# Linear attention and two gated layers on one Trainium2 core: features divided by their denominators before they are turned, and attention products of rounded parts and remainders with up to 512 moving columns

## The chip, the cores and the metric

The kernel runs on one core of a Trainium2 chip. The metric is the device time of one execution in microseconds; before the change it was 1078.28 us, the median of three runs (1075.19 to 1078.71).

## The reference

Attention with random features over 4 batches, 8 heads, 576 tokens, 64 dimensions and 128 features, and then two gated layers over all 2304 tokens (512 wide, 1536 inside), all in float32:

```
def phi(x):
    proj = np.einsum('bhsd,md->bhsm', x, omega)
    h = proj - np.sum(x * x, axis=-1, keepdims=True) / 2.0
    h = h - np.max(h, axis=-1, keepdims=True)
    return np.exp(h) / np.sqrt(m)
q_p, k_p = phi(q * scale), phi(k * scale)
kv = np.einsum('bhsm,bhsd->bhmd', k_p, v)
z = np.sum(k_p, axis=2)
num = np.einsum('bhsm,bhmd->bhsd', q_p, kv)
den = np.einsum('bhsm,bhm->bhs', q_p, z)[..., None] + 1e-06
x = num / den            # then the heads side by side: 2304 tokens x 512
x = (silu(x @ w_gate) * (x @ w_val)) @ w_out
out = ((x @ w_a) * (x @ w_b)) @ w_out2
```

## The kernel before

The 2304 tokens are cut into five chunks: four of 512 and one of 256 tokens. A batch has 576 tokens, so the second chunk holds the last 64 tokens of batch 0 and 448 of batch 1, the third 128 and 384, the fourth 192 and 320, the last one 256 of one batch. Activations lie with the features on the partitions and the tokens as columns, so that each layer's product has the weights as the stationary operand and up to 512 tokens as moving columns.

Precision comes from splitting. A float32 operand is split into a rounded part of the type fp32r (a "hi", written by ScalarE) and the remainder (a "lo", written by VectorE, line 307), and a product of two such operands is three fp32r products: hi by hi, hi by lo and lo by hi (lines 582 to 584). The attention before the change doesn't split its features: there the products of features and key sums are plain fp32 (lines 421 and 486). In the trace a plain fp32 product leaves two records.

`keys` computes, for a batch and a pair of heads, the features of the keys and their product with the values (with a column of ones beside them, so that the last of 65 columns is z): `kvs`. `queries` computes for a chunk and a pair of heads the features of the queries (`qf`), turns them by a transpose on TensorE (line 466) into PSUM, copies them to `fT` (ScalarE, line 469), multiplies each token tile and head by `kvs` (line 486; a tile that crosses from one batch to the next is multiplied by both), adds eps to column 65, takes the reciprocal and scales (VectorE, lines 503, 507, 511) into `xt`, and turns `xt` back (line 519). `put` splits the result into `xh` and `xl`, the first layer's input. `features` is used by both: GpSimd squares the tokens (line 341) and writes the remainder of the projection's input (line 307, tile `rl`); VectorE sums the squares and finds the row maximum; ScalarE takes the exponential.

`weights` provides the stationary operands. In the first chunk (c = 0) each block of weights is rebuilt from 64-bit numbers, by two ScalarE and two VectorE operations (lines 542 to 551), kept in DRAM, and then split (lines 562 and 565). In the later chunks it is loaded and only split. Seven blocks of split weights have buffers.

All instructions are first recorded, each with an engine, a cost, a due time and the tiles that it reads and writes. A planner (class `Plan`) then goes through a modelled time, and on each engine takes, of what is ready, what is due first; tiles of a ring are given out in the order of recording. What comes out is a fixed order on each engine, and an engine stops at an instruction whose inputs are late. The attention of the next chunk is due between two thirds of this chunk's first layer and nine tenths of its second, so the second chunk's attention lies in the first chunk, among its weights' rebuilding. ScalarE has to load a table when it goes from exponential to silu or back.

## Time and profile before

| | |
|---|---|
| median of three runs | 1078.28 us |
| the profiled execution's own time | 1075.15 us |
| its span, first to last instruction | 1073.4 us |
| TensorE busy | 1053.0 us |
| VectorE busy | 659.4 us |
| ScalarE busy | 605.0 us |
| GpSimd busy | 87.5 us |
| granted clock of TensorE | 1.00 |

TensorE's busy time is made of instructions that overlap, so a full engine says that it always had one under way, and not how fast they followed each other; the chain of waits, which counts each instruction from the end of the one before it, tells the pace. Shares of the whole span hide that the first chunk, up to about 290 us, differs from what follows: there the weights are rebuilt.

### The profile page before, as it was taken

Reading aid. Unit: us, or ns where it says so; the run is one execution under the profiler, and the core shown is the slowest. Engines: PE = TensorE matmul, PEld = TensorE weight load, DVE = VectorE, ACT = ScalarE, POOL = GpSimd, SP = SyncE. Lnnn points to the kernel's source line nnn. Section 1 sums busy time; section 2 is a strip of 40 time slices with the busy share of each in tenths; the row PEclk is TensorE's granted clock in tenths of the full one; section 3 lists DMA queues with packets and bytes.
Section 4 is the critical chain, followed back from the end, with each engine's and each line's share of the span. In section 5 each row is a group of like instructions: output and inputs, shape, how many; then the busy total and the mean of one; then the engine's idle time right before and its main releaser. Section 6 shows DMA issues by size and latency. Waiting matters only on the chain.

```text
span 1073.4 us, 15791 instructions
## 1 busy us (share of the span) xinstructions
PE 1053.0 (98%) x5596; PEld 900.6 (84%) x5596; DVE 659.4 (61%) x1266; ACT 605.0 (56%) x1212; POOL 87.5 (8%) x73
## 2 busy tenths in 40 slices
...
GB/s 269 247 274 239 259 310 259 277 281 257 186 108 98 89 133 103 101 125 132 118 99 95 101 93 101 84 73 104 112 97 101 96 89 90 89 118 183 183 184 99
DMA packets 113263, 162.59 MB, mean 151 GB/s; under 512 B 30112, under 2 KB 53280, under 8 KB 113184
## 3 DMA queue, kind: packets, MB, share of 16 engines
...
q14 instruction: 35, 0.29, 0.1%
HBM read 137.95 MB, written 23.59 MB: 151 GB/s over the span
## 4 chain that ended last, share of the span: by engine, by line
PE 80%; DVE 12%; ACT 5%; issue 2%; DMA 1%; POOL 0%; SPq 0%; ACTq 0%; DVEq 0%; POOLq 0%
PE ps_m L582 24%; PE ps_m L584 23%; PE ps_m L583 23%; PE ps_p L373 3%; DVE w L548 2%; PE ps_t L486 2%; DVE wl L307 2%; PE ps_kv L421 2%; DVE w L551 2%; DVE mx L379 1%; PE ps_t L466 1%; ACT w L545 1%; ACT w L542 1%; DVE s L346 1%; ACT wh L562 1%
## 5 line engine op out<-in xcount | busy, mean ns | idle before, releaser
L307 DVE TENSOR_TENSOR wl<-w,wh 128x512 fp32r<-128x512 f32 x360 | 258.6, 720 | 247.6 <-ACT wh L562 242.4
L582 PE MATMUL ps_m<-xh,wh 128*128 128x512 f32 (+1 forms) x960 | 360.1, 375 | 3.1 <-ACT wh L562 1.2
L583 PE MATMUL ps_m<-xl,wh 128*128 128x512 f32 (+1 forms) x960 | 353.8, 369 | 0.8 <-DVE xl L307 0.8
L584 PE MATMUL ps_m<-xh,wl 128*128 128x512 f32 (+1 forms) x960 | 354.4, 369 | 0.1
L562 ACT ACTIVATE wh<-w 128x512 fp32r<-128x512 f32 x360 | 226.0, 631 | 177.7 <-PE ps_m L583 134.4
L582 PEld LDWEIGHTS ps_m<-xh,wh 128*128 128x128 f32 x960 | 181.3, 189 | 31.0 <-ACT a L600 1.6
L584 PEld LDWEIGHTS ps_m<-xh,wl 128*128 128x128 f32 x960 | 181.0, 189 | 31.2 <-DVE wl L307 0.5
L583 PEld LDWEIGHTS ps_m<-xl,wh 128*128 128x128 f32 x960 | 181.3, 189 | 28.6 <-DVE xl L307 1.2
L582 PE MATMUL ps_m<-hh,wh 128*128 128x512 f32 (+1 forms) x480 | 181.4, 378 | 0.0
L584 PE MATMUL ps_m<-hh,wl 128*128 128x512 f32 (+1 forms) x480 | 177.6, 370 | 0.2 <-DVE wl L307 0.2
L583 PE MATMUL ps_m<-hl,wh 128*128 128x512 f32 (+1 forms) x480 | 177.0, 369 | 0.0
L600 ACT ACTIVATE a<-ps_m 128x512 f32<-128x512 f32 (+1 forms) x120 | 66.7, 556 | 98.2 <-PE ps_m L584 97.6
L603 DVE TENSOR_TENSOR h<-a,ps_m 128x512 f32<-128x512 f32 (+1 forms) x120 | 75.8, 632 | 60.2 <-PE ps_m L584 54.0
L584 PEld LDWEIGHTS ps_m<-hh,wl 128*128 128x128 f32 x480 | 90.5, 189 | 16.7 <-DVE wl L307 1.1
L582 PEld LDWEIGHTS ps_m<-hh,wh 128*128 128x128 f32 x480 | 90.7, 189 | 13.0 <-ACT wh L562 0.2
L583 PEld LDWEIGHTS ps_m<-hl,wh 128*128 128x128 f32 x480 | 90.7, 189 | 13.0
L606 ACT ACTIVATE hh<-h 128x512 fp32r<-128x512 f32 (+1 forms) x120 | 70.9, 591 | 26.6 <-DVE h L603 24.6
L307 DVE TENSOR_TENSOR hl<-h,hh 128x512 fp32r<-128x512 f32 (+1 forms) x120 | 77.9, 649 | 7.1 <-ACT hh L606 2.1
L307 POOL TENSOR_TENSOR rl<-qT,rh 128x512 fp32r<-128x512 f32 (+1 forms) x16 | 20.4, 1275 | 615.1 <-ACT rh L354 516.3
L393 ACT ACTIVATE qf<-ps_p,bias 128x128 f32<-128x128 f32 x144 | 42.3, 377 | 29.7 <-DVE bias L387 29.5
L379 DVE TENSOR_REDUCE mx<-ps_p 128x4 f32<-128x512 f32 (+1 forms) x72 | 46.1, 641 | 16.0 <-PE ps_p L373 15.4
L548 DVE SCALAR_TENSOR_TENSOR w<-w 128x512 uint32<-128x512 uint32 x72 | 51.8, 725 | 6.6 <-ACT w L545 6.4
...
## 6 DMA issues: line engine op xcount, KB each, us to landing
...
```

The lines of the kernel that those rows point to most:

```text
L307: eng.tensor_tensor(out=out, in0=a, in1=hi.bitcast(F32), op=ALU.subtract)
L373: nc.tensor.matmul(out, lhsT=w, rhs=x, start=j == 0, stop=j == len(terms) - 1)
L379: on(DVE, dve(256 * n), d, lambda ps=ps, mx=mx, n=n: nc.vector.tensor_reduce(out=mx.tile[:, 0:n], in_=ps.tile.rearrange("p (t h m) -> p t ...
L393: nc.scalar.activation(out=f.tile[:, g + i, h], in_=ps.tile[:, 256 * i + M * h:256 * i + M * (h + 1)], func=AF.Exp, scale=qk_scale, bias=b ...
L548: on(DVE, dve(CW), due - 9, lambda: nc.vector.scalar_tensor_tensor(out=raw.tile[:, :, 0], in0=raw.tile[:, :, 1], scalar=0x80000000, in1=ra ...
L562: on(ACT, act(CW), due - 7, lambda: nc.scalar.activation(out=hi.tile.rearrange("p a c -> p (a c)"), in_=w.tile, func=AF.Copy), reads=[(w,) ...
L582: nc.tensor.matmul(o, lhsT=hi.tile[:, wi], rhs=a, start=first, stop=False)
L583: nc.tensor.matmul(o, lhsT=hi.tile[:, wi], rhs=b, start=False, stop=False)
L584: nc.tensor.matmul(o, lhsT=lo.tile[:, wi], rhs=a, start=False, stop=last)
L600: on(ACT, act(n, 0, True), due, lambda a=a, ps=ps: nc.scalar.activation(out=a.tile[:, 0:n], in_=ps[0].tile[:, 0:n], func=AF.Silu if m == 0 ...
L603: on(DVE, dve(n), due, lambda a=a, h=h, ps=ps: nc.vector.tensor_tensor(out=h.tile[:, 0:n], in0=a.tile[:, 0:n], in1=ps[1].tile[:, 0:n], op= ...
L606: on(ACT, act(n), due + 2, lambda h=h, hh=hh: nc.scalar.activation(out=hh.tile[:, 0:n], in_=h.tile[:, 0:n], func=AF.Copy), reads=[(h,)], w ...
```

## The change

From the second chunk on (`split` is true) `queries` goes to a new function `shared`; the first chunk keeps the way of before (`own`, which now turns the features by head and borrows its tiles from other rings). In `shared`, z is first widened for each batch and pair (`widen`): a column of z, repeated 128 times, is transposed on TensorE, so that z stands in a row on all partitions (`zb`). GpSimd multiplies the features by `zb` (`weigh`), VectorE sums the products to the denominator, adds eps and takes the reciprocal, and GpSimd multiplies the features by it in place. Only then are they turned, each head's four tiles into one PSUM tile, and split into `fh` (ScalarE) and `fl` (VectorE). The key sums are split too (`kp`, with a block of zeros between the two heads, so that a stationary operand of 128 columns holds one head and zeros). Six fp32r products for each batch add both heads into one PSUM tile that has the layout of x, with the batch's tokens of the chunk as moving columns. No transpose of the result follows.

Buffers change with it: keys' and queries' inputs share three tiles; the squares are written over the tokens; the layers' temporaries `a`, `h` and `o` share three tiles; `hh` and `hl` have one tile less. The planner's cost of an fp32 product of 65 columns goes from 0.15 to 0.233.

```diff
--- before.py
+++ after.py
@@ -246,17 +246,16 @@
     ps_k = ring("ps_kv", 1, [P, 512], space=PSUM)
 
     ones = Fixed(None)
+    zeros = Fixed(None)
     ident = fixed("ident", [P, P])
     bd = fixed("bd", [P, 2 * M])
     bdh = fixed("bdh", [P, 2 * M], F32R)
     bdl = fixed("bdl", [P, 2 * M], F32R)
 
-    r_kT = ring("kT", 2, [P, S])
+    r_kT = r_qT = ring("xT", 3, [P, S])
     r_kt = ring("kt", 1, [P, KT, P])
-    r_qT = ring("qT", 2, [P, NT])
     r_qt = ring("qt", 1, [P, NT // P, P])
     r_vt = ring("vt", 2, [P, KT, 2, VA])
-    r_sq = ring("sq", 1, [P, KT, 2, D])
     r_s = ring("s", 3, [P, KT, 2])
     r_nsq = ring("nsq", 3, [P, KT, 2])
     r_rh = ring("rh", 1, [P, S], F32R)
@@ -267,17 +266,18 @@
     r_kf = ring("kf", 1, [P, KT, 2, M])
     r_qf = ring("qf", 2, [P, NT // P, 2, M])
     r_kvs = ring("kvs", 9, [P, 2, VA])
-    r_fT = ring("fT", 1, [P, 2, NT])
-    r_den = ring("den", 3, [P, 2, 2])
-    r_rec = ring("rec", 3, [P, 2, 2])
-    r_xt = ring("xt", 1, [P, NT // P, 2, D])
+    r_zb = ring("zb", 9, [P, 2, M])
+    r_kp = ring("kp", 2, [P, 2, 3, D], F32R)
+    r_fh = ring("fh", 2, [P, NT], F32R)
+    r_fl = ring("fl", 2, [P, NT], F32R)
+    r_pr = ring("pr", 1, [P, 2, 2, M])
+    r_den = ring("den", 3, [P, NT // P, 2])
+    r_rec = ring("rec", 3, [P, NT // P, 2])
     r_xh = ring("xh", 9, [P, NT], F32R)
     r_xl = ring("xl", 9, [P, NT], F32R)
-    r_a = ring("a", 2, [P, NT])
-    r_h = ring("h", 2, [P, NT])
-    r_hh = ring("hh", NF + 1, [P, NT], F32R)
-    r_hl = ring("hl", NF + 1, [P, NT], F32R)
-    r_o = ring("o", 2, [P, NT])
+    r_a = r_h = r_o = ring("tmp", 3, [P, NT])
+    r_hh = ring("hh", NF, [P, NT], F32R)
+    r_hl = ring("hl", NF, [P, NT], F32R)
     r_w64 = ring("w64", 4, [P, CW, 2], U32)
     r_w32 = ring("w32", 4, [P, CW])
     r_wh = ring("wh", 7, [P, NG, P], F32R)
...
@@ -337,15 +340,15 @@
     def features(rT, tok, nt, step, f, due, length, split, psum):
 
         width = step * (nt - 1) + P
-        sq, s, nsq = r_sq.buf(), r_s.buf(), r_nsq.buf()
-        on(POOL, pool(nt * P), due - 4, lambda: nc.gpsimd.tensor_tensor(
-            out=sq.tile[:, 0:nt].rearrange("p t h d -> p (t h d)"),
-            in0=tok.tile[:, 0:nt].rearrange("p t c -> p (t c)"),
-            in1=tok.tile[:, 0:nt].rearrange("p t c -> p (t c)"), op=ALU.mult),
-            reads=[(tok,)], writes=[(sq,)])
+        s, nsq = r_s.buf(), r_nsq.buf()
+
+        def square():
+            x = tok.tile[:, 0:nt].rearrange("p t c -> p (t c)")
+            nc.gpsimd.tensor_tensor(out=x, in0=x, in1=x, op=ALU.mult)
+        on(POOL, pool(nt * P), due - 4, square, writes=[(tok,)])
         on(DVE, dve(nt * P), due - 2, lambda: nc.vector.tensor_reduce(
-            out=s.tile[:, 0:nt], in_=sq.tile[:, 0:nt], op=ALU.add, axis=AX.X),
-            reads=[(sq,)], writes=[(s,)])
+            out=s.tile[:, 0:nt], in_=tok.tile[:, 0:nt].rearrange("p t (h d) -> p t h d", h=2),
+            op=ALU.add, axis=AX.X), reads=[(tok,)], writes=[(s,)])
         on(DVE, dve(16), due - 2, lambda: nc.vector.tensor_scalar(
             out=nsq.tile[:, 0:nt], in0=s.tile[:, 0:nt], scalar1=sq_scale, scalar2=None,
             op0=ALU.mult), reads=[(s,)], writes=[(nsq,)])
...
@@ -417,7 +420,7 @@
         for t in range(KT):
             for h in range(2):
                 r = rows[t]
-                on(PE, pe(0.15), due + length * (t + 1) / KT, lambda h=h, t=t, r=r:
+                on(PE, pe(0.233), due + length * (t + 1) / KT, lambda h=h, t=t, r=r:
                    nc.tensor.matmul(kv.tile[:, VA * h:VA * (h + 1)], lhsT=f.tile[0:r, t, h],
                                     rhs=vt.tile[0:r, t, h], start=(t == 0 and h == 0),
...
@@ -427,6 +430,18 @@
         on(ACT, act(2 * VA, 0, True), due + length, lambda: nc.scalar.activation(
             out=out.tile.rearrange("p h c -> p (h c)"), in_=kv.tile[:, 0:2 * VA], func=AF.Copy),
             reads=[(kv,)], writes=[(out,)])
+
+    def widen(b, p, due):
+
+        out, zb, ps = sums[b, p], r_zb.buf(), ps_t.buf()
+        spread[b, p] = zb
+        for h in range(2):
+            on(PE, pe(0.112), due, lambda h=h: nc.tensor.transpose(
+                ps.tile[:, P * h:P * (h + 1)], out.tile[:, h, D:VA].to_broadcast([P, P]),
+                ident.tile), reads=[(out,), (ident,)], writes=[(ps, h)])
+        on(ACT, act(2 * M, 0, True), due, lambda: nc.scalar.activation(
+            out=zb.tile.rearrange("p h m -> p (h m)"), in_=ps.tile[:, 0:2 * M], func=AF.Copy),
+            reads=[(ps, 0, 1)], writes=[(zb,)])
 
     x_of = {}
 
...
@@ -456,20 +471,26 @@
             out=tok.tile[:, 0:nt], in_=bass.AP(q.tensor, q.offset + t0 * DM + p * P,
                                                [[DM, P], [P * DM, nt], [1, P]])),
            writes=[(tok,)])
-        f, fT, xt = r_qf.buf(), r_fT.buf(), r_xt.buf()
+        f = r_qf.buf()
         features(rT, tok, nt, P, f, due, length * 0.5, split, ps_p)
-        for g in range(0, nt, 2):
-            d = due + length * (0.3 + 0.5 * g / nt)
+        (shared if split else own)(c, p, f, due, length)
+
+    def own(c, p, f, due, length):
+
...
@@ -517,9 +539,92 @@
         for t in range(nt):
             parts = [key for key in xt.state if key[0] == t]
             on(PE, pe(0.11), due + length, lambda t=t: nc.tensor.transpose(
-                ps.tile[:, P * t:P * (t + 1)], xt.tile[:, t].rearrange("p h d -> p (h d)"),
+                ps.tile[:, P * t:P * (t + 1)], xt.tile.rearrange("p a b c -> p (a b) c")[:, t],
                 ident.tile), reads=[(xt, *parts), (ident,)], writes=[(ps, t)])
         ps.state[None] = [[w for t in range(nt) for w in ps.state[t][0]], []]
+        put(1, c, p, ps, n, due + length)
+
+    def shared(c, p, f, due, length):
+
+        t0, t1 = spans[c]
+        n = t1 - t0
+        nt = n // P
+        batches = range(t0 // S, (t1 - 1) // S + 1)
+        for b in batches:
+            if (b, p) not in spread:
+                widen(b, p, due)
+        den, rec = r_den.buf(), r_rec.buf()
+        for g in range(0, nt, 2):
+            d = due + length * (0.3 + 0.5 * g / nt)
+            pr = r_pr.buf()
+            parts = [(t, h) for t in (g, g + 1) for h in range(2)]
+            for b in batches:
+                for i, m in ((0, 2),) if t0 + P * (g + 2) <= (b + 1) * S and t0 + P * g >= b * S \
+                        else ((0, 1), (1, 1)):
+                    a = t0 + P * (g + i)
+                    lo_, hi_ = max(a, b * S) - a, min(a + P * m, (b + 1) * S) - a
+                    if hi_ <= lo_:
+                        continue
+                    hi_ = min(hi_, P)
+
+                    def weigh(pr=pr, g=g, i=i, m=m, lo_=lo_, hi_=hi_, b=b):
+                        x = spread[b, p].tile[lo_:hi_]
+                        nc.gpsimd.tensor_tensor(
+                            out=pr.tile[lo_:hi_, i:i + m], in0=f.tile[lo_:hi_, g + i:g + i + m],
+                            in1=bass.AP(x.tensor, x.offset, [x.ap[0], [0, m], *x.ap[1:]]),
+                            op=ALU.mult)
+                    on(POOL, pool(256 * m), d, weigh, reads=[(f, *parts), (spread[b, p],)],
+                       writes=[(pr, (i, b))])
+            on(DVE, dve(512), d, lambda pr=pr, g=g: nc.vector.tensor_reduce(
+                out=den.tile[:, g:g + 2],
+                in_=pr.tile, op=ALU.add, axis=AX.X),
+                reads=[(pr, *pr.state)], writes=[(den, g)])
+            on(DVE, dve(4), d, lambda g=g: nc.vector.tensor_scalar(
+                out=den.tile[:, g:g + 2], in0=den.tile[:, g:g + 2], scalar1=eps, scalar2=None,
+                op0=ALU.add), writes=[(den, g)])
+            on(DVE, dve(32), d, lambda g=g: nc.vector.reciprocal(
+                out=rec.tile[:, g:g + 2], in_=den.tile[:, g:g + 2]),
+                reads=[(den, g)], writes=[(rec, g)])
+            on(POOL, pool(512), d, lambda g=g: nc.gpsimd.tensor_tensor(
+                out=f.tile[:, g:g + 2], in0=f.tile[:, g:g + 2],
+                in1=rec.tile[:, g:g + 2].to_broadcast([P, 2, 2, M]), op=ALU.mult),
+                reads=[(rec, g)], writes=[(f, *parts)])
+        turned = []
+        for h in range(2):
+            d = due + length * (0.5 + 0.2 * h)
+            ps, fh, fl = ps_t.buf(), r_fh.buf(), r_fl.buf()
+            turned.append((fh, fl))
+            for t in range(nt):
+                on(PE, pe(0.112), d, lambda ps=ps, t=t, h=h: nc.tensor.transpose(
+                    ps.tile[:, P * t:P * (t + 1)], f.tile[:, t, h], ident.tile),
+                   reads=[(f, (t, h)), (ident,)], writes=[(ps, t)])
+            on(ACT, act(n, 0, True), d, lambda ps=ps, fh=fh: nc.scalar.activation(
+                out=fh.tile[:, 0:n], in_=ps.tile[:, 0:n], func=AF.Copy),
+                reads=[(ps, *range(nt))], writes=[(fh,)])
+            on(DVE, dve(n), d, lambda ps=ps, fh=fh, fl=fl: sub(
+                nc.vector, fl.tile[:, 0:n], ps.tile[:, 0:n], fh.tile[:, 0:n]),
+                reads=[(ps, *range(nt)), (fh,)], writes=[(fl,)])
+        ps = ps_t.buf()
+        for b in batches:
+            kp, kv = r_kp.buf(), sums[b, p]
+            cols = slice(max(t0, b * S) - t0, min(t1, (b + 1) * S) - t0)
+            width = cols.stop - cols.start
+            on(ACT, act(2 * D), due + length * 0.3, lambda kp=kp, kv=kv: nc.scalar.activation(
+                out=kp.tile[:, 0, 0:3:2], in_=kv.tile[:, :, 0:D], func=AF.Copy),
+                reads=[(kv,), (zeros, *range(2))], writes=[(kp, 0)])
+            on(DVE, dve(2 * D), due + length * 0.3, lambda kp=kp, kv=kv: sub(
+                nc.vector, kp.tile[:, 1, 0:3:2], kv.tile[:, :, 0:D], kp.tile[:, 0, 0:3:2]),
+                reads=[(kv,), (kp, 0), (zeros, *range(2))], writes=[(kp, 1)])
+            for h in range(2):
+                def attend(h=h, kp=kp, cols=cols):
+                    (xh, xl), out = turned[h], ps.tile[:, cols]
+                    hi, lo = (kp.tile[:, i].rearrange("p a d -> p (a d)")[:, D * h:D * h + P]
+                              for i in range(2))
+                    for j, (w, x) in enumerate(((hi, xh), (hi, xl), (lo, xh))):
+                        nc.tensor.matmul(out, lhsT=w, rhs=x.tile[:, cols], start=h + j == 0,
+                                         stop=h == 1 and j == 2)
+                on(PE, pe(3 * max(0.12, FFN * width)), due + length, attend,
+                   reads=[(kp, 0, 1), *((x,) for x in turned[h])], writes=[(ps,)])
         put(1, c, p, ps, n, due + length)
```

On TensorE, the second chunk's first pair of heads before: its products with the sums of batches 0 and 1 (`kvs_105`, `kvs_109`) among the layer's products, and the second half of the feature transposes.

```order
L584 MATMUL ps_m_59<-hh_151,wl_190 128x512
L486 MATMUL ps_t_63<-kvs_105,fT_114 128x65 x2
L486 MATMUL ps_t_63<-kvs_109,fT_114 128x65 x4
L582 MATMUL ps_m_59<-hh_152,wh_184 128x512
L583 MATMUL ps_m_59<-hl_165,wh_184 128x512
L584 MATMUL ps_m_59<-hh_152,wl_191 128x512
L466 MATMUL ps_t_64<-ident_69,qf_103 128x128 x4
L582 MATMUL ps_m_59<-hh_153,wh_184 128x512
L583 MATMUL ps_m_59<-hl_166,wh_184 128x512
```

At the same place after: the products of the turned features' parts (`fh`, `fl`) with the split sums of batch 0 (`kp_121`, 64 columns) and batch 1 (`kp_122`, 448 columns), into one PSUM tile, with a projection's three products between them.

```order
L689 MATMUL ps_m_58<-hh_162,wl_200 128x512
L624 MATMUL ps_t_63<-fh_123,kp_121 128x64
L624 MATMUL ps_t_63<-fl_125,kp_121 128x64
L624 MATMUL ps_t_63<-fh_123,kp_121 128x64
L376 MATMUL ps_p_62<-bdh_71,rh_86 128x256
L376 MATMUL ps_p_62<-bdl_72,rh_86 128x256
L376 MATMUL ps_p_62<-bdh_71,rl_87 128x256
L624 MATMUL ps_t_63<-fh_124,kp_121 128x64
L624 MATMUL ps_t_63<-fl_126,kp_121 128x64
L624 MATMUL ps_t_63<-fh_124,kp_121 128x64
L624 MATMUL ps_t_63<-fh_123,kp_122 128x448
L624 MATMUL ps_t_63<-fl_125,kp_122 128x448
```

The products of each token tile with `kvs` have become products over all tokens of a batch; they stand together, where those of before stood in two groups with layer products between.

On GpSimd, the same pair of heads before: projections' remainders (`rl`) and squares (`sq`) alone.

```order
L307 TENSOR_TENSOR rl_89<-kT_74,rh_88 128x576
L341 TENSOR_TENSOR sq_81<-kt_75 128x640
L307 TENSOR_TENSOR rl_89<-qT_77,rh_88 128x512
L341 TENSOR_TENSOR sq_81<-qt_78 128x512
L307 TENSOR_TENSOR rl_89<-kT_73,rh_88 128x576
```

And after, between the remainder of the queries' projection and that of the next pair's: the features' products with z (`pr`) and their division (`qf` by `rec`).

```order
L307 TENSOR_TENSOR rl_87<-xT_75,rh_86 128x512
L572 TENSOR_TENSOR pr_127<-qf_101,zb_112 64x256
L572 TENSOR_TENSOR pr_127<-qf_101,zb_113 64x256
L572 TENSOR_TENSOR pr_127<-qf_101,zb_113 128x256
L307 TENSOR_TENSOR rl_87<-xT_74,rh_86 128x576
L572 TENSOR_TENSOR pr_127<-qf_101,zb_113 128x512
L588 TENSOR_TENSOR qf_101<-qf_101,rec_133 128x512
L347 TENSOR_TENSOR kt_76<-kt_76 128x640
L588 TENSOR_TENSOR qf_101<-qf_101,rec_133 128x512
L347 TENSOR_TENSOR qt_77<-qt_77 128x512
```

Six instructions have come between those of before, and the next pair's remainder (`rl_87` from `xT_74`) now stands behind three of them.

## Rows read from the trace of the kernel before

In the windows view the columns are the stretch, its length, and for each engine its busy time with the number of its instructions, then the granted clock, the share of the DMA engines and GB/s. In the groups the columns are line, engine, operation, output and inputs with their shapes, the count, busy us, mean ns, and the idle time before with what ended it.

**Rows 1.** The page's list of engines: busy us, share, instructions.
```profile
PE 1053.0 (98%) x5596; PEld 900.6 (84%) x5596; DVE 659.4 (61%) x1266; ACT 605.0 (56%) x1212; POOL 87.5 (8%) x73
```

**Rows 2.** Busy us and instructions of each engine by stretches of the span.
```profile
core 0: us, PE busy (x) PEld busy (x) DVE busy (x) ACT busy (x) POOL busy (x), PEclk, DMA share, GB/s
100.00:130.00 30.00, 28.43 (x134) 22.99 (x133) 22.86 (x39) 29.80 (x47) 0.00 (x0) 1.00 0.73 245
130.00:180.00 50.00, 49.76 (x249) 41.62 (x248) 46.10 (x85) 42.21 (x83) 4.94 (x3) 1.00 0.83 281
180.00:265.00 85.00, 82.92 (x440) 69.64 (x439) 82.62 (x167) 70.10 (x147) 14.27 (x8) 1.00 0.82 274
265.00:280.00 15.00, 15.00 (x81) 12.76 (x80) 13.90 (x29) 10.25 (x24) 3.76 (x3) 1.00 0.79 242
280.00:290.00 10.00, 10.00 (x51) 8.40 (x50) 3.36 (x7) 2.98 (x5) 0.00 (x0) 1.00 0.48 153
290.00:960.00 670.00, 670.00 (x3286) 563.44 (x3286) 340.81 (x631) 307.24 (x609) 38.00 (x32) 1.00 0.34 102
```

**Rows 3.** TensorE's waits, 20 to 290 us: total, times, longest.
```profile
PE ps_kv L421 <- ACT kf L393: 2.9, 7, 0.8
```

**Rows 4.** The chain of waits: start us, us, what.
```profile
41.73 0.87 PE ps_p L373 x4
...
269.43 0.71 PE ps_p L373 x6
...
270.84 0.44 PE ps_t L466 x4
...
280.65 0.84 PE ps_t L486 x8
281.49 0.29 PE ps_m L582
281.77 0.23 PE ps_m L583
```

**Rows 5.** VectorE's groups, 180 to 265 us: busy us, mean ns, idle before.
```profile
L307 DVE TENSOR_TENSOR wl<-w,wh 128x512 fp32r<-128x512 f32 x26 | 20.2, 782 | 0.9 <-ACT wh L562 0.8
L548 DVE SCALAR_TENSOR_TENSOR w<-w 128x512 uint32<-128x512 uint32 x26 | 19.4, 752 | 0.9 <-ACT w L545 0.9
...
L387 DVE TENSOR_TENSOR bias<-nsq,top 128x2 f32<-128x2 f32 x3 | 1.5, 516 | 0.0
L383 DVE SCALAR_TENSOR_TENSOR top<-mx,nsq 128x2 f32<-128x2 f32 x2 | 1.4, 704 | 0.0
L307 DVE TENSOR_TENSOR xl<-ps_t,xh 128x512 fp32r<-128x512 f32 x2 | 1.4, 684 | 0.0
L346 DVE TENSOR_REDUCE s<-sq 128x8 f32<-128x512 f32 x2 | 1.4, 681 | 0.1
...
L511 DVE TENSOR_TENSOR xt<-ps_t,rec 64x128 f32<-64x128 f32 x4 | 1.1, 278 | 0.1
L511 DVE TENSOR_TENSOR xt<-ps_t,rec 128x256 f32<-128x256 f32 x2 | 0.8, 420 | 0.0
...
L507 DVE RECIPROCAL rec<-den 64x2 f32<-64x2 f32 x4 | 0.6, 155 | 0.1
...
L511 DVE TENSOR_TENSOR xt<-ps_t,rec 128x128 f32<-128x128 f32 x2 | 0.6, 292 | 0.1
```

**Rows 6.** In order of time, GpSimd and VectorE at 220 us: start, us, instruction.
```profile
220.19 1.77 POOL L307 TENSOR_TENSOR rl<-qT,rh 128x512 fp32r<-128x512 f32 x1 [23.81 <-ACT rh L354]
...
220.73 1.25 DVE L383 SCALAR_TENSOR_TENSOR top<-mx,nsq 128x2 f32<-128x2 f32 x1
```

**Rows 7.** Groups of GpSimd and ScalarE over the span.
```profile
L341 POOL TENSOR_TENSOR sq<-qt 128x512 f32<-128x512 f32 x16 | 20.9, 1306 | 45.5 <-DVE s L346 37.9 <-DVE bias L387 4.1 <-DMA qt<-q_t 3.5
...
L307 POOL TENSOR_TENSOR rl<-qT,rh 128x256 fp32r<-128x256 f32 x4 | 3.1, 784 | 175.7 <-ACT rh L354 175.7
...
L393 ACT ACT_TABLE_LOAD x12 | 15.4, 1283 | 15.7 <-DVE bias L387 15.6
```

36 lines of the change are left out of this document (22 added, 14 removed).

## The prediction

> **What bounds the kernel now.** I read the page first, then the busy time by stretches, TensorE's waits, the chain of waits, and VectorE's groups. The page shows TensorE busy for 98% of the span [rows 1]. By stretches, it is busy for all 670 us between 290 and 960 us, while VectorE is busy for half of that time (340.81 of 670) and GpSimd for 38 us [rows 2]. There only TensorE's own work counts: a matmul less is time less. The chain of waits, which counts every instruction from its predecessor's end, gives TensorE's real pace: 0.23 us for a product of 512 columns, 0.71 us for six fp32r products of 256 columns (0.118 each), 0.44 us for four transposes (0.11 each) [rows 4]. An fp32 product with 65 columns leaves two records in the trace, so the group of eight is four products: 0.84 us, and the product behind it takes 0.29 us where its neighbour takes 0.23, so (0.84 + 0.06) / 4 = 0.225 us each. An fp32 product of 256 columns also leaves two records: 0.87 / 2 = 0.435 us [rows 4].
>
> Before 290 us it is another kernel. That is the first chunk, in which every weight is also rebuilt from its 64-bit form, and in which the second chunk's attention is computed. VectorE is busy 46.10 of 50 us from 130 to 180, 82.62 of 85 from 180 to 265 and 13.90 of 15 up to 280, and only after that it has air (3.36 of 10) [rows 2]. So from 130 to 280 us it has 3.9 + 2.4 + 1.1 = 7.4 us of idle time. TensorE is nearly full in the same stretch, but not quite: from 180 to 265 it lacks 2.1 us, and the largest of its waits between 20 and 290 us was for key features that came late, 2.9 us in 7 waits [rows 2, 3].
>
> **The change on TensorE.** For a pair of heads, before: transposes of the features, one fp32 product for each head and token tile (two more where a tile crosses a batch border), and transposes of the result. After: the same feature transposes, two transposes for each batch to widen its sums (counted where the batch is new), and six fp32r products for each batch in the chunk, as wide as its share of the chunk; the transposes of the result go. Per pair, with the paces above:
> Second chunk (shares of 64 and 448 columns): before 8 x 0.11 + 10 x 0.225 + 4 x 0.11 = 3.57. After 0.88 + 4 x 0.11 + 6 x (0.118 + 0.20) = 3.23. Saved 0.34.
> Third (128 and 384): before 0.88 + 8 x 0.225 + 0.44 = 3.12. After 0.88 + 0.22 + 6 x (0.17 + w).
> Fourth (192 and 320): before 3.57. After 0.88 + 0.22 + 6 x (0.144 + w).
> Fifth (256 tokens): before 0.44 + 0.90 + 0.22 = 1.56. After 0.44 + 6 x 0.118 = 1.15. Saved 0.41.
> The open price is w, an fp32r product of 128 or 192 columns: no row has one. From below it is the 0.118 of 256 columns, from above fp32's pace, 0.435 x 128/256 = 0.22 and 0.435 x 192/256 = 0.33 [rows 4]. I take the nearest row in columns: 128 is nearer to 65 columns (0.225) than to 256, so 0.22; 192 is nearer to 256, so 0.118. The third chunk then takes 3.44 (0.32 more), the fourth 2.67 (0.90 less). For four pairs: third +1.3, fourth -3.6, fifth -1.6, together -3.9 us in stretches where TensorE alone counts. With 0.118 for both it is -1.2 - 3.6 - 1.6 = -6.4, with fp32's pace for both +1.3 + 1.4 - 1.6 = +1.1. The second chunk's 4 x 0.34 = 1.4 us lies before 290 us, where VectorE sets the pace, and I count it as slack.
>
> **The change on VectorE and GpSimd, in the first chunk.** For each pair of the second chunk VectorE loses two scaled evictions, one of them in three pieces (2 x 0.278 + 0.292 + 0.420 = 1.27), and eight small operations of 0.155; it gains two sums over 512 elements (0.681 each), two remainders of the turned features (0.684 each), two splits of the key sums (like the 0.292) and four small ones. Net 2.73 + 0.58 - 1.27 - 0.62 = 1.42 us, 5.7 us for four pairs [rows 5].
> GpSimd gets six new instructions per pair, three of 512 elements and three of 256 or on half the partitions: 24 in this stretch. The rows show what such an instruction does to VectorE. At 220.73 us a VectorE operation on two columns took 1.25 us where others of its kind take 0.15; it ended at 221.98, and GpSimd's operation that began at 220.19 had ended at 221.96 [rows 6]. Summed over 180 to 265 us, against 0.684 for 512 elements and 0.155 for a small operation: 26 x 0.098 + 26 x 0.068 + 3 x 0.36 + 2 x 0.55 = 6.5 us lost to 8 GpSimd operations, 0.81 each [rows 2, 5]. The 12 long new ones cost 12 x 0.81, the 12 short ones 12 x 0.81 x 784/1306 [rows 7], together 15.6 us.
> The Trainium skill says why (SBUF — State Buffer, "Who interferes with whom"): a VectorE instruction with two SBUF inputs and a GpSimd instruction that reads SBUF exclude each other for the whole of the instruction. The rows agree, and it speaks against this change.
> So VectorE has 5.7 + 15.6 = 21.3 us more to do where 7.4 us are idle. If TensorE is held up by all that doesn't fit, that is 13.9 us. From below: of the 6.5 us that VectorE lost from 180 to 265 us TensorE lost 2.1, a third, because weights are split ahead; a third of 15.6 is 5.0, and the 5.7 fits in the idle time. I take the middle, 9.5 us.
> ScalarE's order has two table loads fewer in this chunk, 2 x 1.283 us, and ScalarE was busy 29.80 of 30 us from 100 to 130 [rows 2, 7]. From below nothing, from above 2.6 less; I take 1.3 less.
>
> **What I cost at nothing.** After 290 us GpSimd and VectorE get the same additions, covered by VectorE's idle half [rows 2]; should that cover fail, transposes and attention products stand in TensorE's fixed order ahead of the layers' products, and each late one stops these. Two key and two query buffers become three shared ones, six temporaries three, and a spare remainder buffer goes: an up-projection step holds two temporaries and lasts 24 x 0.23 = 5.5 us, against VectorE operations of 0.7. At the start VectorE's order has two weights' splits ahead of the first x remainder that stood behind it, six instructions of some 0.7 us; they fill time in which it waits for data, or shift the start by up to 4 us either way.
>
> **Sum.** The profiled execution took 1075.15 us (span 1073.4 and 1.75 around it). 1075.15 + 9.5 - 1.3 - 3.9 = 1079.5. The median of the three runs is 3.1 us above the profiled execution, and the runs spread over 3.5 us; moved by that, 1082.6, so 1083 us, 0.4% slower.
>
> **Rivals.**
> TensorE's saving carries it: VectorE's extra work before 290 us goes into idle time and into the weights' lead (of the 6.5 us lost before, two thirds didn't reach TensorE), and narrow products run at 0.118. 1078.3 - 6.4 - 1.3 = 1070.6, and 1069 if the second chunk's 1.4 comes too. For it: TensorE at 670 of 670 us. Against it: no idle VectorE to speak of.
> A wash: TensorE loses only the third, 5.0, with narrow products as I took them: 1078.3 + 5.0 - 1.3 - 3.9 = 1078. Or the saving comes whole and VectorE's stretch costs what it saves. For it: TensorE's 2.1 us of loss under eight GpSimd operations.
> The full lock: every GpSimd operation stops VectorE for all of its time, 12 x 1.306 + 12 x 0.784 = 25.1 us. Then 25.1 + 5.7 - 7.4 = 23.4, and 1078.3 + 23.4 - 1.3 - 3.9 = 1096. It decides from the point at which VectorE has next to it nothing that reads PSUM. Against it: the measured 0.81 is less than the mean 1.78 of those eight operations, as sums over PSUM went on beside them [rows 2].
> That the change doesn't do what it says is ruled out by the order: the transposes of the result are gone from the second chunk on.
>
> **How the numbers follow.** My forecast (1081 to 1088) has a chance of 0.36, the wash 0.26, TensorE's saving 0.22, the full lock 0.16. A measurement of this kernel tells about 0.3%, 3.2 us, from no change. Faster than that: the saving and a bit of the wash, 0.24. Within it: the rest of the wash and the forecast's lower edge, 0.32. Slower: 0.44. Range: the saving's 1070 to a lock of nearly full strength, 1094; the forecast's own range is 1079 to 1088.
>
> **What would show it.** By my steps the profile after has GpSimd operations of 0.8 to 1.3 us (24 of them) between 120 and 290 us, VectorE idle for less than 3 us from 130 to 280, weight splits there above 0.78 us, and the second chunk's layers begin 5 to 9 us later than before. Behind that its chunks are shorter by 0.9 us a pair in the fourth and 0.4 in the fifth; a product of 128 columns shows w directly. It is wrong if TensorE shows no new waits before 290 us, or if it shows waits at feature transposes after 290 us, which I cost at nothing.

## The result: 1.2% slower

The changed kernel takes 1089.89 us in the median of four runs (1085.10 to 1092.77); the kernel before, run beside it, 1076.74. The ratio is 1.0121, 95% interval 1.0101 to 1.0140. The forecast was 1083 us with a range of 1070 to 1094 and "slower" as the likeliest: direction and range held, but the loss is 13.2 us against the kernel beside it where the forecast's own sum has 4.3. The size was wrong.

The page of the profile after (span; busy time; TensorE's granted clock in 40 slices of 27.3 us, 9 standing for 0.9 or more):

```profile
span 1091.0 us, 15787 instructions
...
PE 1060.8 (97%) x5484; PEld 901.6 (83%) x5484; DVE 698.8 (64%) x1278; ACT 616.1 (56%) x1258; POOL 169.9 (16%) x151
...
PEclk9899989999999999999999999999999999999999
```

The clock row is new. Before the change the mean granted clock was 1.00, here it is 0.987 in the profiled execution, with an 8 in two slices of the first chunk and, by stretches, 0.93 and 0.96 (the columns are those of [rows 2]):

```profile
130.00:180.00 50.00, 45.64 (x214) 37.27 (x213) 43.95 (x76) 37.23 (x77) 11.52 (x10) 0.93 0.80 269
180.00:265.00 85.00, 77.58 (x381) 63.57 (x380) 82.39 (x144) 67.03 (x143) 25.67 (x19) 0.96 0.75 249
130.00:280.00 150.00, 138.22 (x669) 113.63 (x668) 140.67 (x246) 115.84 (x244) 38.23 (x30) 0.95 0.75 253
290.00:960.00 670.00, 667.58 (x3220) 558.24 (x3219) 371.62 (x658) 318.08 (x646) 101.45 (x91) 1.00 0.35 104
```

Against [rows 2]: TensorE lacks 4.4 us from 130 to 180 and 7.4 from 180 to 265, where it lacked 0.2 and 2.1. VectorE, with 82.39 of 85, is as full as it was there, and GpSimd does 25.67 us instead of 14.27. From 130 to 280 us as a whole VectorE is idle for 9.3 us, more than the 7.4 of before: TensorE loses time though VectorE is not fuller. What TensorE waited for (engine, line, releaser: us in total, times, longest):

```profile
PE ps_t L598 <- POOL qf L588: 8.6, 11, 1.9
...
PE ps_t L541 <- DVE pr L532: 4.3, 4, 1.4
PE ps_t L624 <- DVE fl L307: 2.8, 2, 1.8
...
PE ps_kv L424 <- ACT kf L396: 1.3, 2, 1.2
```

The transposes of the divided features (L598) wait for GpSimd's division, and the attention products (L624) for VectorE's remainders; 7.0 of the 8.6 us lie before 320 us. The 4.3 us for `pr` (L541) lie between 20 and 62 us: `own` keeps the first chunk's scaled result in a `pr` tile, and before the change TensorE waited 1.1 us for that result. A stop can cost more than its length. TensorE's instructions in order of time behind one of them (start, us, instruction, idle time before):

```profile
259.69 0.66 PE L598 MATMUL ps_t<-ident,qf 128*128 128x128 f32 x4 [1.91 <-POOL qf L588]
260.10 0.63 PE L687 MATMUL ps_m<-xh,wh 128*128 128x512 f32 x1
260.53 0.63 PE L688 MATMUL ps_m<-xl,wh 128*128 128x512 f32 x1
...
263.09 0.63 PE L688 MATMUL ps_m<-xl,wh 128*128 128x512 f32 x1
```

Behind a stop of 1.91 us, products of 512 columns start 0.43 us apart where 0.23 is their pace [rows 4]: TensorE runs at 1.2 instead of 2.4 GHz from 260.3 to 263.7 (granted clock 0.50).

The first layer product of the second chunk, before and after, tells how much of the loss is made until then:

```profile
295.49 0.39 PE L582 MATMUL ps_m<-xh,wh 128*128 128x512 f32 x1
```

```profile
316.29 0.39 PE L687 MATMUL ps_m<-xh,wh 128*128 128x512 f32 x1
```

That is 20.8 us. The busy times up to these two starts, and in the stretches at half clock before 316 us (five in all; the first two are shown, and the sum of the five):

```profile
0.00:295.49 295.49, 278.32 (x1444) 232.80 (x1445) 255.54 (x517) 235.33 (x479) 49.47 (x41) 1.00 0.80 260
```

```profile
0.00:316.29 316.29, 290.99 (x1412) 240.85 (x1413) 268.48 (x510) 237.61 (x494) 76.03 (x68) 0.96 0.73 241
```

```profile
28.20:35.00 6.80, 6.80 (x28) 6.03 (x28) 5.69 (x9) 4.47 (x15) 2.79 (x2) 0.50 0.55 185
52.10:58.90 6.80, 5.80 (x20) 4.91 (x21) 6.80 (x19) 4.61 (x14) 1.52 (x2) 0.50 0.85 286
...
sum 27.20, PE 25.66 PEld 21.67 DVE 24.50 ACT 18.12 POOL 5.35; mean PE 5.13 PEld 4.33 DVE 4.90 ACT 3.62 POOL 1.07
```

TensorE is idle for 25.3 us instead of 17.2, 8.1 more, and of 27.2 us at half clock it is busy for 25.7, which costs up to 12.8 us. Together that is about the whole 20.8 us: in this execution the clock can account for more of it than the waits themselves. Read in the same way, the third chunk begins at 548.61 instead of 527.27 us, the fourth at 779.96 instead of 760.87, the fifth at 983.93 instead of 966.34. So computing the third chunk's attention (inside the second) costs 0.5 us, the fourth's saves 2.2, the fifth's 1.5, together 3.2 us saved in these executions. The whole loss lies in the first chunk. This profiled execution is the slowest of the four; by the medians the first chunk loses 13.2 + 3.2 = 16.4 us.

### The profile page after: what moved, and what is told of

Read it like the earlier page. It is cut to its first block, busy times and chain, and to the rows that moved or that the text cites. A ratio compares the mean times of both kernels' runs of the same rounds, so it can differ in the third digit from the quotient of the medians.

```text
span 1091.0 us, 15787 instructions
## 1 busy us (share of the span) xinstructions
PE 1060.8 (97%) x5484; PEld 901.6 (83%) x5484; DVE 698.8 (64%) x1278; ACT 616.1 (56%) x1258; POOL 169.9 (16%) x151
## 4 chain that ended last, share of the span: by engine, by line
PE 69%; DVE 2%; POOL 1%; DMA 1%; issue 0%; ACT 0%; POOLq 0%; ACTq 0%
PE ps_m L687 21%; PE ps_m L689 21%; PE ps_m L688 21%; PE ps_p L376 2%; PE ps_t L624 2%; PE ps_kv L424 1%; PE ps_t L598 1%; DMA kt<-k_t 1%; POOL qf L588 1%; POOL pr L572 1%; DVE wl L307 0%; DVE den L578 0%; DVE top L386 0%; POOL kt L347 0%; DVE s L349 0%
## 5 line engine op out<-in xcount | busy, mean ns | idle before, releaser
L307 DVE TENSOR_TENSOR wl<-w,wh 128x512 fp32r<-128x512 f32 x360 | 266.8, 743 | 231.6 <-ACT wh L667 217.7
L307 POOL TENSOR_TENSOR rl<-xT,rh 128x576 fp32r<-128x576 f32 (+2 forms) x28 | 37.3, 1331 | 577.6 <-ACT rh L357 576.6
L705 ACT ACTIVATE tmp<-ps_m 128x512 f32<-128x512 f32 (+1 forms) x120 | 66.6, 556 | 92.0 <-PE ps_m L689 89.7
L708 DVE TENSOR_TENSOR tmp<-tmp,ps_m 128x512 f32<-128x512 f32 (+1 forms) x120 | 75.7, 631 | 58.1 <-PE ps_m L689 52.0
L687 PEld LDWEIGHTS ps_m<-hh,wh 128*128 128x128 f32 x480 | 91.2, 190 | 13.2
L711 ACT ACTIVATE hh<-tmp 128x512 fp32r<-128x512 f32 (+1 forms) x120 | 70.7, 589 | 30.9 <-DVE tmp L708 28.7
L307 DVE TENSOR_TENSOR hl<-tmp,hh 128x512 fp32r<-128x512 f32 (+1 forms) x120 | 82.3, 686 | 5.8 <-ACT hh L711 1.2
L572 POOL TENSOR_TENSOR pr<-qf,zb 64x256 f32<-64x256 f32 (+2 forms) x48 | 51.4, 1077 | 73.4 <-ACT qf L396 69.9
L396 ACT ACTIVATE kf<-ps_p,bias 128x128 f32<-128x128 f32 x120 | 36.2, 368 | 36.8 <-DVE bias L390 26.2
```

Of the source, the lines that this page charges most:

```text
L307: eng.tensor_tensor(out=out, in0=a, in1=hi.bitcast(F32), op=ALU.subtract)
L396: nc.scalar.activation(out=f.tile[:, g + i, h], in_=ps.tile[:, 256 * i + M * h:256 * i + M * (h + 1)], func=AF.Exp, scale=qk_scale, bias=b ...
L572: nc.gpsimd.tensor_tensor(out=pr.tile[lo_:hi_, i:i + m], in0=f.tile[lo_:hi_, g + i:g + i + m], in1=bass.AP(x.tensor, x.offset, [x.ap[0], [ ...
L687: nc.tensor.matmul(o, lhsT=hi.tile[:, wi], rhs=a, start=first, stop=False)
L705: on(ACT, act(n, 0, True), due, lambda a=a, ps=ps: nc.scalar.activation(out=a.tile[:, 0:n], in_=ps[0].tile[:, 0:n], func=AF.Silu if m == 0 ...
L708: on(DVE, dve(n), due, lambda a=a, h=h, ps=ps: nc.vector.tensor_tensor(out=h.tile[:, 0:n], in0=a.tile[:, 0:n], in1=ps[1].tile[:, 0:n], op= ...
```

## The experiments

The theory after the result (A): the loss is made in the first chunk, because TensorE, in its fixed order, stops for results of GpSimd and VectorE. Within it, A1: VectorE, blocked by GpSimd, is late; A2: the new chain (feature product, sum, reciprocal, division) is longer than the order allows. Rivals: B, the new products cost more by themselves; C, VectorE has too much work in the first chunk, whatever the order. D, E and F came up on the way. "Second chunk at" is the start of its first layer product in the profiled execution: 295.5 us before, 316.3 after.

**e1: the old way for the second chunk.**

```
-        (shared if split else own)(c, p, f, due, length)
+        (shared if c > 1 else own)(c, p, f, due, length)
```

(The old way is `own`, with the features turned by head. It gets its own two tiles for turned features, and `zb` five tiles instead of nine.)

> The second chunk's attention, computed in the first chunk, goes the old way; the new way from the third chunk on. Theory A (the loss is made in the first chunk, where TensorE in its fixed order stops for results of GpSimd and VectorE and then also runs at the lower clock): the second chunk's layers begin at about 295 us as before, the granted clock is 1.00 from 100 us on, and of the change the later chunks' saving is left, 3 to 4 us: ratio to before 0.996 to 0.998. Rival B (the new products and transposes themselves cost more than the old ones, in every chunk): three quarters of the loss stay, ratio 1.008 or more.

Measured: 1082.45 us, ratio 1.0061 (1.0048 to 1.0075), second chunk at 303.1 us, fifth at 971.0. Busy times from 130 to 260 us:

```profile
130.00:180.00 50.00, 46.13 (x241) 38.29 (x240) 46.50 (x89) 40.22 (x83) 5.69 (x4) 1.00 0.84 288
180.00:260.00 80.00, 77.04 (x402) 63.70 (x401) 76.65 (x152) 64.05 (x133) 11.77 (x8) 1.00 0.83 272
```

B is out: about half the loss goes with the new attention in the first chunk alone. The clock is 1.00 here. But the chunk is still 7.6 us late, which theory A didn't expect: something else in the changed kernel, outside the new attention, costs time too.

**e2: GpSimd's work without its chain, in the kernel before.** Six multiplications of the features for each pair of heads in the second chunk, their results unused:

```
+        if c == 1:
+            for g in range(0, nt, 2):
...
+                for i, m in ((0, 2), (0, 2)) if g else ((0, 1), (1, 1), (0, 1), (0, 2)):
+                    e = r_ex.buf()
+                    on(POOL, pool(256 * m), d, lambda e=e, g=g, i=i, m=m: nc.gpsimd.tensor_tensor(
+                        out=e.tile[:, i:i + m], in0=f.tile[:, g + i:g + i + m],
+                        in1=f.tile[:, g + i:g + i + m], op=ALU.mult),
+                       reads=[(f, *parts)], writes=[(e,)])
```

> The kernel before, with 24 GpSimd multiplications of the features' sizes (12 of 512, 12 of 256 elements) in the second chunk's attention, that nothing waits for. Theory A1 (it is the blocking of VectorE by GpSimd that makes VectorE's results late for TensorE): TensorE waits more before 300 us and the second chunk begins 4 to 9 us later, with some time at the lower clock; ratio 1.004 to 1.010. Theory A2 (TensorE waits for the new chain itself, feature product, sum, reciprocal, division, which is longer than the order allows): nothing is in that chain here, VectorE's blocking goes into its idle time, ratio 1.000 to 1.003.

Measured: 1086.10 us, ratio 1.0098 (1.0084 to 1.0111), second chunk at 305.2 us. No engine waits for a result of these 24 instructions, and the second chunk starts 9.7 us later, 0.40 us for each. TensorE's waits between 20 and 320 us; VectorE's groups from 180 to 265 us, before and here; the busy times in that stretch and up to the second chunk's start:

```profile
PE ps_t L530 <- DVE xt L522: 6.0, 4, 3.5
PE ps_kv L422 <- ACT kf L394: 3.0, 5, 1.7
```

```profile
L307 DVE TENSOR_TENSOR hl<-h,hh 128x512 fp32r<-128x512 f32 x11 | 7.5, 684 | 0.0
L603 DVE TENSOR_TENSOR h<-a,ps_m 128x512 f32<-128x512 f32 x11 | 7.5, 679 | 0.0
...
L387 DVE TENSOR_TENSOR bias<-nsq,top 128x4 f32<-128x4 f32 x8 | 1.2, 156 | 0.0
```

```profile
L308 DVE TENSOR_TENSOR wl<-w,wh 128x512 fp32r<-128x512 f32 x23 | 18.5, 813 | 0.1
...
L308 DVE TENSOR_TENSOR hl<-h,hh 128x512 fp32r<-128x512 f32 x10 | 9.6, 956 | 0.0
L614 DVE TENSOR_TENSOR h<-a,ps_m 128x512 f32<-128x512 f32 x10 | 6.8, 679 | 0.5 <-PE ps_m L595 0.5
...
L388 DVE TENSOR_TENSOR bias<-nsq,top 128x4 f32<-128x4 f32 x8 | 3.3, 410 | 0.0
```

```profile
180.00:265.00 85.00, 78.12 (x408) 65.47 (x407) 81.84 (x155) 65.14 (x136) 27.25 (x20) 0.98 0.76 250
0.00:305.20 305.20, 282.61 (x1444) 235.22 (x1445) 264.44 (x517) 235.15 (x479) 77.27 (x65) 0.99 0.78 252
```

Operations with two SBUF inputs have grown (`hl` from 684 to 956 ns, `bias` from 156 to 410), one that reads PSUM has not (`h`, 679 in both). VectorE's 517 instructions up to the second chunk's start take 264.4 us instead of 255.5, 8.9 more. TensorE's wait for the scaled result, VectorE's work, has grown from 1.1 to 6.0 us (L530); that for the key features (3.0) is as before. A changed order isn't the cause of most of it: TensorE's order is that of before but for three places where key products stand a few instructions apart, VectorE's is the same up to what started at 227 us before, and by then TensorE is already late (the product that started at 217.61 us starts at 223.53). A1 holds for the kernel before: its ratio is at the upper end of what was expected, its place 0.7 us beyond it. That the new chain costs nothing in the changed kernel (A2) is not shown by it.

**e3: the same chain on VectorE.** In `shared`, both GpSimd operations become VectorE's:

```
-                        nc.gpsimd.tensor_tensor(
+                        nc.vector.tensor_tensor(
...
-                    on(POOL, pool(256 * m), d, weigh, reads=[(f, *parts), (spread[b, p],)],
+                    on(DVE, dve(256 * m), d, weigh, reads=[(f, *parts), (spread[b, p],)],
...
-            on(POOL, pool(512), d, lambda g=g: nc.gpsimd.tensor_tensor(
+            on(DVE, dve(512), d, lambda g=g: nc.vector.tensor_tensor(
```

> The changed kernel with the products with z and the division on VectorE instead of GpSimd, everywhere. It takes the blocking away and shortens the chain, and adds about 6 x 0.6 us to VectorE for a pair of heads. Theory A1 (blocking): VectorE has 12 x 0.6 + 12 x 0.3 = 11 us more to do and is blocked for 15.6 less, the second chunk begins some 3 to 8 us earlier than in the changed kernel; ratio to before 1.003 to 1.010. Theory A2 (length of the chain through GpSimd): the waits at the feature transposes go, ratio near 1.000. Rival C (VectorE's capacity in the first chunk, however its work is cut): as slow as the changed kernel, 1.010 to 1.015.

Measured: 1083.55 us, ratio 1.0074 (1.0060 to 1.0089), second chunk at 305.8 us. Busy times up to it:

```profile
0.00:305.76 305.76, 284.53 (x1412) 236.15 (x1413) 271.18 (x534) 237.34 (x494) 47.56 (x44) 0.98 0.77 249
```

VectorE is busy for 271.2 us, where the changed kernel has 268.5, and the kernel is faster, so C is out. By the ratios it is 5.1 us faster than the changed kernel (1.0121 less 1.0074), within A1's 3 to 8 us; that its second chunk begins 10.5 us earlier is more, because the changed kernel's profiled execution is its slowest. The chain is shorter here and GpSimd's blocking is gone, both at once, so this run doesn't tell A1 from A2. TensorE waits 3.0 us for the division here, where it waited 7.0 in the changed kernel.

**e4: GpSimd's results later in the plan.**

```
-        return dict(pace=0.2 + n * 0.0023)
+        return dict(pace=0.2 + n * 0.0023, lat=1.7 + n * 0.0023)
```

> The changed kernel, with the planner told that every GpSimd result comes 1.5 us later than it was told; the instructions are the same, and only their order differs. Theory A (stops because results come later than the order supposes): the transposes stand some 12 layer products later, most of the 7 us of waits for the division before 300 us goes and with it the time at the lower clock; the second chunk begins 8 to 15 us earlier than in the changed kernel, ratio to before 0.998 to 1.004. Rival C (VectorE's capacity in the first chunk): the order can't help, 1.010 to 1.015.

Measured: 1096.46 us, ratio 1.0193 (1.0176 to 1.0210), the slowest of all; second chunk at 320.1 us. Its waits from 20 to 320 us:

```profile
PE ps_t L624 <- DVE fl L307: 8.4, 3, 3.2
PE ps_t L598 <- POOL qf L588: 5.1, 5, 1.5
```

The waits for the division fell only from 7.0 to 5.1 us, and the wait moved on to the remainders (8.4, from 2.8). This expectation failed. The extra delay is told of every GpSimd result, squares and projections' remainders among them, so it moves much more than the transposes; which of these moves cost the time, no run separates.

**e5 and e6: what else the change brought.** e5 is the kernel before with the planner's new cost alone:

```
-                on(PE, pe(0.15), due + length * (t + 1) / KT, lambda h=h, t=t, r=r:
+                on(PE, pe(0.233), due + length * (t + 1) / KT, lambda h=h, t=t, r=r:
...
-                        on(PE, pe(0.15), d, lambda ps=ps, g=g, i=i, h=h, b=b, col=col:
+                        on(PE, pe(0.233), d, lambda ps=ps, g=g, i=i, h=h, b=b, col=col:
```

e6 is the kernel before with the new buffers alone:

```
-    r_kT = ring("kT", 2, [P, S])
+    r_kT = r_qT = ring("xT", 3, [P, S])
...
-    r_a = ring("a", 2, [P, NT])
-    r_h = ring("h", 2, [P, NT])
+    r_a = r_h = r_o = ring("tmp", 3, [P, NT])
-    r_hh = ring("hh", NF + 1, [P, NT], F32R)
-    r_hl = ring("hl", NF + 1, [P, NT], F32R)
+    r_hh = ring("hh", NF, [P, NT], F32R)
+    r_hl = ring("hl", NF, [P, NT], F32R)
```

> The kernel before with nothing but the planner's cost of an fp32 product of 65 columns changed from 0.15 to 0.233, as the change has it. The old attention in the first chunk of the changed kernel (e1) was still 7.6 us late at the second chunk's start, with VectorE as full as before. Theory D (the lower cost made the planner put TensorE's work too early, so that TensorE came to each result late enough not to wait; with the true cost it comes in time and waits for VectorE's delays): second chunk at 299 to 304 us, ratio 1.003 to 1.008. Rival E (it is the shared buffers): ratio 0.999 to 1.001.

> The kernel before with the change's buffers alone: three tiles for keys' and queries' inputs, three for the layers' temporaries, one tile less for hh and hl; costs and attention as before. Theory E (the shared buffers delay the start and the weights' rebuilding): first layer products at 50 us or later, second chunk at 299 to 304 us, ratio 1.003 to 1.008. Rival D (the planner's cost): ratio 0.999 to 1.001.

Measured: e5 1082.26 us, ratio 1.0054 (1.0042 to 1.0067), second chunk at 301.9 us. e6 1075.71 us, ratio 0.9997 (0.9987 to 1.0008), second chunk at 295.6 us. E falls: the buffers cost nothing, though they change the order too. D's numbers hold: the number 0.233, which is close to the 0.225 that such a product takes [rows 4], costs the kernel before 6 us. TensorE's waits of e5 between 20 and 320 us:

```profile
PE ps_t L466 <- ACT qf L393: 4.6, 3, 1.8
PE ps_kv L421 <- ACT kf L393: 4.0, 5, 1.4
```

Feature transposes that waited 0.2 us for exponentials before now wait 4.6, all of it before 62 us, in the first chunk's own attention; the 4.0 us for key features, where 2.0 were waited before, lie behind 130 us, in the second chunk's. In each of the two places the granted clock falls to 0.50 once, at 43.7 and at 146.1 us. That the low cost let TensorE lag its plan, and so arrive late enough, fits this; the lag itself was not measured.

**e7 and e8: the old cost in the changed kernel and in e1.** In both, `pe(0.233)` goes back to `pe(0.15)` at its two places.

> The changed kernel with the planner's cost of the fp32 products back at 0.15. Theory D: the second chunk begins 3 to 8 us earlier than in the changed kernel, and with fewer stops less time is spent at the lower clock; ratio to before 1.003 to 1.008. Theory E: no change from the changed kernel, 1.010 to 1.014.

> The old attention for the second chunk, the new one from the third on, and the planner's cost back at 0.15. Theory D: the first chunk as before, the later chunks' saving of 3 to 4 us left, ratio 0.996 to 0.998, faster than both kernels. Theory E: as the same kernel with 0.233, 1.005 to 1.007.

Measured: e7 1088.68 us, ratio 1.0115 (1.0101 to 1.0128), second chunk at 312.2 us; by the ratios 0.6 us faster than the changed kernel, less than the intervals can tell. e8 1079.55 us, ratio 1.0033 (1.0021 to 1.0046), second chunk at 303.3 us; by the ratios 3.0 us faster than e1. Both miss what D expected: the 6 us that the cost takes from the kernel before come back by half in e8 and hardly at all in the changed kernel. In e8, TensorE waited 3.8 us in 9 waits for exponentials at the old way's transposes, which the change had regrouped by head.

**e9 and e10: a faster kernel?** e9 gives the first two chunks the old way with the transposes two tiles at a time, as before the change, with cost 0.15, and `shared` from the third chunk on. e10 is e9 with later GpSimd results in `shared` alone:

```
-                    on(POOL, pool(256 * m), d, weigh, ...
+                    on(POOL, dict(pace=0.2 + 256 * m * 0.0023, lat=0.7 + 256 * m * 0.0023), d, weigh, ...
-            on(POOL, pool(512), d, lambda g=g: nc.gpsimd ...
+            on(POOL, dict(pace=1.378, lat=2.378), d, lambda g=g: nc.gpsimd ...
```

> The first two chunks' attention exactly by the old way (features turned two tiles at a time, planner's cost 0.15), the new way from the third chunk on. In e8, where the old way turned the features by head, TensorE waited for exponentials at these transposes (3.8 us in 9 waits before 320 us) and the second chunk began at 303.25 us. Theory F (that turning by head is the rest of e8's loss): the second chunk begins at 295 to 298 us, ratio 0.995 to 0.998, faster than both kernels. Rival: as e8, 1.002 to 1.004.

> As e9, with the planner told that the feature products and divisions on GpSimd take 0.5 and 1 us longer to come. If the third chunk's missing saving (0.5 us lost where 1.2 to be saved) lies in stops at feature transposes, these go and another 1 to 2 us are saved against e9: ratio 0.994 to 0.997. If the order puts other late things there, as it did in e4, it is no faster than e9.

Measured: e9 1075.56 us, ratio 0.9996 (0.9987 to 1.0005), second chunk at 297.2 us, fifth at 964.7 (966.3 before). e10 1074.70 us, ratio 0.9988 (0.9975 to 1.0001). F holds for the place (297.2), but both miss the ratios that were expected (0.995 to 0.998, 0.994 to 0.997), and neither is measurably faster than the kernel before. The later chunks save 3.4 us in e9's profiled execution and 5.4 in e10's, 2.0 more, the upper end of what was expected; e10's second chunk begins at 301.9 us in it, so its first chunk takes that back.

e7 and e9 have the same cost and differ in the first two chunks' attention and its tiles alone (the new way in the second chunk and turning by head in the first, against the old way in both). Between them lie 1.0115 and 0.9996, 12.8 us: nearly all that the changed kernel loses. How much of it belongs to the first chunk's turning by head, no run separates.

**e11: what a stop costs.** In the kernel before, one transpose in each of three chunks waits for GpSimd squares that the planner takes for nothing:

```
+            if m == 0 and f == 3 and c in (1, 2, 3):
+                ex, pt = r_ex.buf(), ps_t.buf()
+                for j in range((1, 2, 4)[c - 1]):
+                    x = ex if j else a
+                    on(POOL, dict(pace=0.05), due, ...
+                on(PE, pe(0.11), due, lambda ex=ex, pt=pt: nc.tensor.transpose(
+                    pt.tile[:, 0:P], ex.tile[:, 0:P], ident.tile),
+                   reads=[(ex,), (ident,)], writes=[(pt,)])
```

> The kernel before with three single stops of TensorE, in the second, third and fourth chunk's first layer, where it has no other waits: one transpose each, which waits for a chain of one, two and four GpSimd squares of 512 elements that begins when an activation is done, and that the planner takes for nothing. It measures a stop by itself. If a stop costs only its length, each of these chunks is longer by the stop that the trace shows, and the granted clock stays 1.00. If a stop also lowers the clock, the chunk with the longest stop shows a granted clock below 1.00 behind it and is longer by 1 to 4 us more than its stop; a short stop may cost its length alone.

Measured (one execution, 1088.64 us). TensorE around the three stops, in order of time; the idle time is in brackets:

```profile
319.07 0.33 PE L611 MATMUL ps_t<-ident,ex 128*128 128x128 f32 x1 [0.51 <-POOL ex L608]
319.15 0.48 PE L583 MATMUL ps_m<-xh,wh 128*128 128x512 f32 x1
319.47 0.39 PE L584 MATMUL ps_m<-xl,wh 128*128 128x512 f32 x1
319.70 0.39 PE L585 MATMUL ps_m<-xh,wl 128*128 128x512 f32 x1
```

```profile
553.18 0.33 PE L611 MATMUL ps_t<-ident,ex 128*128 128x128 f32 x1 [1.95 <-POOL ex L608]
553.26 0.48 PE L583 MATMUL ps_m<-xh,wh 128*128 128x512 f32 x1
...
554.11 0.63 PE L583 MATMUL ps_m<-xh,wh 128*128 128x512 f32 x1
...
556.67 0.63 PE L583 MATMUL ps_m<-xh,wh 128*128 128x512 f32 x1
```

```profile
792.89 0.48 PE L611 MATMUL ps_t<-ident,ex 128*128 128x128 f32 x1 [4.19 <-POOL ex L608]
793.02 0.78 PE L583 MATMUL ps_m<-xh,wh 128*128 128x512 f32 x1
793.59 0.63 PE L584 MATMUL ps_m<-xl,wh 128*128 128x512 f32 x1
...
795.73 0.63 PE L583 MATMUL ps_m<-xh,wh 128*128 128x512 f32 x1
...
796.46 0.39 PE L585 MATMUL ps_m<-xh,wl 128*128 128x512 f32 x1
```

Behind 0.51 us the products go on 0.23 us apart. Behind 1.95 us they are 0.43 us apart from 554.1 to 557.1, behind 4.19 us from 793.6 to 796.2. The three chunks that hold the stops took 0.9, 3.9 and 6.1 us longer than in the kernel before: the stop, and 0.4, 1.9 and 1.9 us beside it. The short stop costs little more than itself, each of the longer ones some 2 us more. The stretches at half clock, and for comparison a stop in e12 (below) with the stretch behind it:

```profile
554.00:557.40 3.40, 3.40 (x9) 2.62 (x9) 1.68 (x3) 1.26 (x2) 0.00 (x0) 0.50 0.07 25
792.90:796.30 3.40, 3.40 (x9) 2.72 (x10) 0.33 (x1) 0.63 (x1) 0.00 (x0) 0.50 0.00 0
```

```profile
256.83 0.44 PE L530 MATMUL ps_t<-ident,xt 128*128 128x128 f32 x2 [2.71 <-DVE xt L522]
```

```profile
256.80:262.00 5.20, 5.17 (x27) 4.47 (x28) 5.20 (x9) 3.99 (x8) 0.00 (x0) 1.00 0.98 332
```

A stop of 2.71 us left the clock at 1.00. So the length of a stop doesn't settle whether the clock falls: e11 has another fall, from 113.7 us, behind a stop of 1.23 us that in the kernel before (at 110.67) is just as long and has none behind it. What decides stays open; each of the two falls shown cost some 2 us.

**e12: both causes in the kernel before.** e2 with `pe(0.233)`.

> The kernel before with both: the planner's cost of 0.233 and the 24 GpSimd multiplications that nothing waits for. Alone they put the second chunk's start at 301.9 and 305.2 us instead of 295.5. If they add, it begins at 309 to 313 us and the ratio to before is 1.013 to 1.017; then, less the later chunks' saving of 3 to 4 us, they make up the changed kernel's loss of 1.0121. If both draw on the same slack, the second chunk begins at 305 to 308 us, ratio 1.009 to 1.012, and 4 us or more of the changed kernel's first chunk belong to something else, its longer chain.

Measured: 1088.43 us, ratio 1.0110 (1.0092 to 1.0128), second chunk at 308.0 us. Of 6.4 and 9.7 us, 12.5 are there together: they overlap in part, the second of the two cases that were expected. By the medians it loses 11.2 us, so of the changed kernel's 16.4 us in the first chunk about 5 are left, and more if the cost counts for as little there as in e7. Its chain is longer (VectorE's own additional work, the stops at L598 and L624), its first chunk's own attention waits more (L541), and it spends more time at the lower clock; how the rest divides between these stays open.

## Why the prediction was wrong

**What was right.** The place and the cause of the loss: GpSimd's work in the first chunk lengthens VectorE's, and TensorE waits for it; e2 shows it alone, in the kernel before. Two table loads fewer came as forecast; what they are worth no run shows.

**The step that failed is the price of the first chunk.** I set 9.5 us, the middle of 5.0 and 13.9, less 1.3 for table loads; it is 16.4 by the medians. I had worked it out as an overflow: so much more work for VectorE, less its idle time. The rows don't bear that out. Up to the second chunk's start VectorE is busy for 12.9 us more (268.5 against 255.5), not 21.3; it keeps 9.3 us of idle time from 130 to 280; and e3, with more on VectorE, is faster. By these rows it counted when single results came in TensorE's fixed order, and not how much VectorE had to do in all. Four things are in the wrong price.
The blocking: I worked out 15.6 us on VectorE for the 24 instructions, of which a third would reach TensorE at the least. e2 has 8.9 us on VectorE, and TensorE's second chunk 9.7 us late: 5.4 us more idle time (305.2 less 282.6, against 17.2), and a clock of 0.99 instead of 1.00 up to there. The price was too high and the share that comes through too low, and the two errors nearly cancel.
The clock: I counted a wait by its length and a fall of the clock at nothing. In the changed kernel's profiled execution the falls cost up to 12.8 us before 316 us, against 8.1 us of more waiting. Its four runs order by it: spans of 1083.3, 1085.6, 1090.6 and 1091.0 us at mean clocks of 0.995, 0.994, 0.989 and 0.987. So in the faster of them the falls took less.
The first chunk's own attention: the diff turns its features by head and borrows tiles, and the prediction has no term for it. TensorE's wait for its result grows from 1.1 to 4.3 us, and two of the five falls of the clock lie there. e9, with the transposes as before, still has a fall at 26.2 us, so which edit brings them stays open.
The planner's cost: the diff shows 0.15 becoming 0.233, and the prediction has no term for it either. In the kernel before it is worth 6 us alone (e5) and about 3 beside the blocking (e12), but in the changed kernel taking it back gives 0.6 us, which is noise (e7). So it is no shown part of the 16.4 us.

**The open price w** was at its lower end for both widths. Twelve products of the third chunk's attention and twelve of the fourth's, in the chain of waits (start, us, what):

```profile
418.86 1.72 PE ps_t L624 x12
```

```profile
650.87 1.55 PE ps_t L624 x12
```

Six of 384 columns at 0.17 leave 0.12 for one of 128; six of 320 at 0.141 leave 0.12 for one of 192. "The nearest row in columns" chose wrongly for 128: it was an fp32 row, and the type decided. With w = 0.118 the later chunks' sum is -6.4 (third -1.2, fourth -3.6, fifth -1.6), and +0.5, -2.2 and -1.5 came. That the 3.2 us saved are near the 3.9 of the forecast is luck: two errors, w and the lateness after 290 us that I had cost at nothing, cancel. TensorE waits 2.4 us in 5 waits for the division after 290 us (1.6 of it after 320), which the prediction named as a sign that it is wrong; the rest is not accounted for. e10, whose plan expects these results later, saves 5.4 of the 6.4 us. So that less work is less time after 290 us held by half.

**The rivals.** The full lock, at 1096, is nearer in size to the result than the forecast but gives the wrong reason for it: blocking alone cost 9.7 us, not 23. Of the signs that the prediction named, waits before 290 us and the second chunk's late start came, by 20.8 us and not by 5 to 9. Others failed: VectorE is idle for 9.3 us from 130 to 280, not for less than 3; the weights' splits there take 0.72 us from 180 to 265, not over 0.78 (the `hl` remainders grew instead, from 684 to 838 ns); 18 of the 24 new GpSimd operations lie before 290 us, with 0.7 to 1.8 us each. The start shifted by more than the 4 us that were allowed, first layer product at 54.6 instead of 46.3 us; but the layer product that started at 136.3 us before starts at 137.0, so in layer products the two kernels are nearly level there.
